# A retention layer and two MLPs on one core: the first loads throttled to 1 MB under way, two weight tiles decoded by halves, half of the first products moved ahead of the last attention, evacuations in pairs

## The chip, the cores and the metric

The kernel runs on one core of a Trainium2 chip. The metric is the device time of one launch in microseconds (us). Before the change it is 880.4 us, the median of three runs (880.11 to 880.4).

## The reference, cut to what matters

```
scores = q k^T / sqrt(64)                      # batch 4, 8 heads, 576 positions, head 64, f32
ret    = scores * gamma_h^(i-j) for j <= i     # a decay in place of a softmax
x      = (ret v) as 2304 tokens x 512
h = x @ moe_w_in;   x = max(0.01 h, h) @ moe_w_out        # 512 -> 2048 -> 512
h = x @ moe2_w_in;  out = (h * sigmoid(h)) @ moe2_w_out
```

q, k, v and x are f32; the four weight matrices arrive as 64-bit numbers and are decoded to f32 on the core.

## The kernel before, in words

**Engines.** PE is the matrix engine, DVE the vector engine, ACT the scalar engine, POOL a third elementwise engine; SP only issues DMAs. Each runs its own list in order, so an instruction that waits holds up all that stands behind it on its engine. The first part of the program, up to the end of the first two token blocks (`FIXED` steps), keeps the order in which it is written; what comes later is ordered by a scheduler.

**Attention.** The tokens of each of the four batches are cut into a unit A (256) and a unit B (320). A unit is worked off in two groups g of two head pairs p: `scale_k` multiplies a copy of the keys by decays, `products` makes the small 64x64 products (tile `r`: scores and key-value sums), DVE masks them (`pt`) and chains the states (`first`, `st`, `sa`), `outer` and `values` make the output (tile `o`), and DVE writes it to `X`. Units u0 = A of batch 0 and u1 = A of batch 1 come ahead of everything else (lines 449 to 509). They are the 512 tokens of the first block. Their q, k, v arrive as 16 loads of 256 KB (`qkvk`). The six other units are spread between the steps of the MLP; `attend` issues their parts when the step counter has passed a due time, and their loads (`qkv`, 672 KB each for a unit B) have due times too (0.3, 0.8 and 1.3 steps for the first three).

**MLP.** A block of up to 512 tokens is worked off in 16 steps, one for each tile f of 128 hidden units. At step t PE makes `gemm1` of tile t (12 products of 128x512 into `h`: hi and lo parts of x and of the weight in three passes over four chunks c) and `gemm2` of tile t-2 (12 products into `acc`). A product needs its operands split in two: `xs`, `wi`, `wo`, `g` each hold a part "hi" (a cast on ACT) and a part "lo" (a subtraction on DVE, for a few on POOL). The second product of a pass group needs the lo part of x or g, the third the lo part of the weight.

**Weights.** A tile f of both matrices is 1 MB in 64-bit form, loaded into one of three buffers `w64` by two DMAs of 512 KB. `decode` turns it into f32: ACT (line 319), DVE (324, 334), ACT again for a share `by_act` of the columns (330), DVE (337, 340). In block 0, at step t ACT and DVE decode tile t+2, split its `wi` half, make g of tile t and split `wo` of tiles t-1 and t. In order on ACT: 319, the activation `hs` of step t, 330, `g`, `wi`, `wo`. On DVE: 324, 334, 337, the lo part of `wo`, 340, then the lo parts of `g` and `wi`. A `w64` buffer is loaded again when the decode of the tile in it is over.

**Fillers.** `busy` issues products whose result nobody reads.

Of the kernel before, what the change touches and what calls it, by code (L numbers as in the profile page):

```python
# [24 lines left out]
BUSY = 3  # L25
# [39 lines left out]
def retention_mlp_kernel(ctx: ExitStack, tc: tile.TileContext, qkva, qkvb, w1, w2, consts, out):  # L65
# [76 lines left out]

    def load(u, p):

        k, b = u
        n, nv = (CA, 2) if k == "A" else (CB, 3)
        nq = n + 128 * nv
        m = nq + 128 * (nv + 2)
        src = (qkva if k == "A" else qkvb)[b, p]
        if u in UNITS[:2]:  # L150

            t = wraw_p.tile([128, m], F32, tag="wraw", name="qkvk")
            nc.sync.dma_start(out=t[:, :nq], in_=src[:, :nq])
            nc.sync.dma_start(out=t[:, nq:], in_=src[:, nq:])
        else:
            t = ld_p.tile([128, 1344], F32, tag="ld", name="qkv")
            nc.sync.dma_start(out=t[:, :m], in_=src)
        vk = t[:, nq:m].rearrange("p (k h d) -> p k h d", h=2, d=64)
        raw[u, p] = t[:, :n], t[:, n:nq], vk[:, :nv], vk[:, nv:]
# [11 lines left out]
    def products(u, ps):  # L171
# [23 lines left out]
        for p in ps:  # L195
            pt = pt_p.tile([128, 2, nm, CH], F32, tag="pt", name="pt")
            nc.vector.tensor_tensor(
                out=pt, in0=s[p].rearrange("p j (m n) -> p j m n", n=CH),
                in1=mask[:, 2 * p:2 * p + 2].unsqueeze(2).to_broadcast([128, 2, nm, CH]), op=ALU.mult)
# [21 lines left out]
        if first:  # L221
            last[u, ps] = t[:, 1, o:o + 256].rearrange("p (i n) -> p i n", i=2)[:, :, 64:]

# [71 lines left out]
    def load_w(layer, f):  # L295

        if layer == 1 and f < 2:
            w = ld_p.tile([128, 1024], F32, tag="ld", name="wraw")
        else:
            w = wraw_p.tile([128, 1024], F32, tag="wraw", name="wraw")  # L300
        wraw[layer, f] = w
        r = dec_p.tile([128, 1024, 2], I32, tag="w64", name="w64")
        src = (w1, w2)[layer][f].bitcast(I32)
        halves = [slice(0, 512), slice(512, 1024)]
        loads = []
        for c in halves:
            loads.append(nc.sync.dma_start(out=r[:, c].rearrange("p n t -> p (n t)"), in_=src[:, 2 * c.start:2 * c.stop]))
        for c in halves if (layer, f) == (0, 0) else [slice(0, 1024)]:
            wdec.append((w[:, c], r[:, c]))
        return loads[0]  # L310
# [32 lines left out]
    def split_wi(layer, i, f):  # L343

        w = wi_p.tile([128, 2, 512], F32R, tag="wi", name="wi")
        wsp[layer, i, f, 0] = w
        return split(w[:, 0], w[:, 1], wraw[layer, f][:, :512], nc.gpsimd if (layer, i, f) == (0, 0, 0) else nc.vector)
# [42 lines left out]
    def gemm2(layer, i, f):  # L390
        p0, n = BLOCKS[layer][i]
        nt = KC if layer == 0 else n // 128
        if f == 0:
            t = [acc_p.tile([128, 2, 512], F32, tag=f"acc{m}", name=f"acc{m}") for m in range((nt + 1) // 2)]
            acc[layer, i] = [t[m // 2][:, m % 2] for m in range(nt)]
        g, w = gs[layer, i, f], wsp[layer, i, f, 1]
        for m in range(nt):
            a = acc[layer, i][m]
            ms = slice(m * 128, (m + 1) * 128)
            for wa, ga in PASSES:  # L400
                st = f == 0 and (wa, ga) == (0, 0)
# [5 lines left out]
            if f < NF - 1:  # L407
                yield
                continue
            if layer == 0:  # L410
                if m % 2:
                    nc.vector.tensor_copy(out=X[:, m, p0:p0 + n], in_=a[:, :n])
                else:
                    nc.scalar.copy(out=X[:, m, p0:p0 + n], in_=a[:, :n])  # L414
            else:
                y = y_p.tile([128, 512], F32, tag="y", name="y")
                if m % 2:
                    nc.vector.tensor_copy(out=y, in_=a)  # L418
                else:
                    nc.scalar.copy(out=y, in_=a)  # L420
                for o, ln, r in rows_of(p0 + m * 128, 128):
                    nc.sync.dma_start(out=out[r:r + ln], in_=y[o:o + ln])
            yield


    nw = 0

    def more_weights(upto, x=None):
        nonlocal nw
        while nw < min(upto, 2 * NF):  # L430
            y = load_w(nw // NF, nw % NF)
            if x is not None:
                behind(y, x)
                x = None
            nw += 1

    def decodes():
        while wdec:
            run(decode(*wdec.pop(0)))
# [3 lines left out]
    nc.vector.memset(warm[:, :1], 0.0)  # L443
# [4 lines left out]
    ordered.enter_context(tc.manual_schedule())  # L448
    u0, u1 = UNITS[:2]
    nc.sync.dma_start(out=cst, in_=consts)  # L450
    more_weights(1)
    for g in range(NG):
        for u in (u0, u1):
            for p in (2 * g, 2 * g + 1):
                load(u, p)
    nc.vector.tensor_tensor(
        out=mask, in0=mask, in1=gn_sb.unsqueeze(2).to_broadcast([128, H, CH]), op=ALU.mult)
    decodes()
    more_weights(2)
# [5 lines left out]
    def sums(u, g):  # L465
        products(u, (2 * g, 2 * g + 1))

    t = ps_p.tile([128, 512], F32, tag="ps", name="busy")

    def busy(n):  # L470

        for _ in range(n):
            mm(t[:, :256], mask[:, 0:2], mask[:, 0:4], True, True)
# [7 lines left out]
    leave(u0, (0, 1))  # L481
    outer(u0, 0)
    values(u0, 0)
    sums(u1, 0)
    leave(u1, (0, 1))
    outer(u1, 0)
    sums(u0, 1)
    leave(u0, (2, 3))
    x = values(u1, 0)

    more_weights(4, x)
    for c in range(2):
        split_x(0, 0, c)
    outer(u0, 1)
    busy(1)
    sums(u1, 1)
    second = decode(*wdec.pop(0), 1024)
# [8 lines left out]
    busy(BUSY)  # L506
    for c in range(2, KC):
        split_x(0, 0, c)
    leave(u1, (2, 3))
# [5 lines left out]
    for u, a, z in ATT:  # L515
# [20 lines left out]
    for t, (l, i, f) in enumerate(steps):  # L536
        first = t < FIXED
        if t == 0:
            run(second)
            more_weights(5)  # L540
            run(split_wi(*steps[1]))
        for n, _ in enumerate(gemm1(l, i, f)):
            attend(t + (n + 1) / 8)
        a = activate(l, i, f)
        if first:

            d = decode(*wdec.pop(0), 512) if t + 2 < NF else iter(())
# [26 lines left out]
        if first:  # L574
            run(wi)
            if ends_block:
                next(wo)
# [15 lines left out]
        if t == FIXED - 1:  # L593
            ordered.close()
# [62 lines left out]
```

## Time and profile before

| | |
|---|---|
| median of 3 runs | 880.4 us |
| profiled execution, its own time | 880.94 us |
| span of its records | 879.2 us |
| PE busy | 855.6 us (97%) |
| DVE busy | 535.3 us (61%) |
| ACT busy | 442.8 us (50%) |
| bytes read from HBM | 53.09 MB |

How to read it: PE is the engine that everything ends on, and its share is an average. The first 80 us (attention of two units, then the block in which the weights are decoded) are a stage of their own, in which DVE, ACT and the DMA queue are busy too; behind it PE has next to no gap. Matrix products overlap each other, so the time of one (its latency) is longer than the distance between two.

### The profile page before, as it was taken

The numbers are of one execution on the slowest core, as the hardware profiler recorded it, in microseconds if no ns is written. First come the engines' busy times: TensorE is split into PE (matmuls) and PEld (weight loads), VectorE is DVE, ScalarE is ACT, GpSimd is POOL, SyncE is SP. The second block draws the span as 40 slices with busy tenths as digits, with TensorE's granted clock in tenths as the row PEclk, the third lists the DMA queues.
The fourth block names the chain that finished last, engine by engine and source line by source line (L and its number), as shares of the span: only waits on it lengthen the run. The fifth ranks groups of instructions, "written<-read, shape, count | busy, mean of one in ns | idle before, by whom it ended". The sixth has DMA issues, their size and how long they took to land.

```text
span 879.2 us, 14579 instructions
## 1 busy us (share of the span) xinstructions
PE 855.6 (97%) x6000; PEld 717.5 (82%) x6000; DVE 535.3 (61%) x928; ACT 442.8 (50%) x766; POOL 10.5 (1%) x27
## 2 busy tenths in 40 slices
PE   4899999999999999999999999999999999999997
PEld 4578778998877877888999888888888888888896
DVE  4688875576455564446999554654465445544575
ACT  2687754454333443445666444544454445444564
POOL 2100000000000000000000000000000000000000
PEclk9999999999999999999999999999999999999999
DMA  7576541221012010101561000010001000100010
GB/s 294 205 258 229 186 160 57 87 83 57 1 59 87 24 52 30 48 1 48 193 238 49 1 0 1 1 48 1 1 1 48 1 0 1 48 1 0 25 25 25
DMA packets 17826, 58.75 MB, mean 67 GB/s; under 512 B 2016, under 2 KB 2144, under 8 KB 17760
## 3 DMA queue, kind: packets, MB, share of 16 engines
q1 hardware_dynamic: 17760, 57.82, 18.8%
q8 instruction: 47, 0.77, 0.4%
q14 instruction: 19, 0.16, 0.1%
HBM read 53.09 MB, written 4.72 MB: 66 GB/s over the span
## 4 chain that ended last, share of the span: by engine, by line
PE 91%; DVE 1%; ACT 1%; issue 0%; DVEq 0%
PE acc L129 44%; PE h L129 43%; PE o L129 2%; PE r L129 2%; DVE wraw L340 0%; ACT X L414 0%; DVE st L231 0%; DVE g L108 0%; DVE y L418 0%; ACT g L107 0%; ACT wo L107 0%; DVE wi L108 0%; ACT hs L384 0%; ACT y L420 0%; DVE xs L108 0%
## 5 line engine op out<-in xcount | busy, mean ns | idle before, releaser
L129 PE MATMUL h<-xs,wi 128*128 128x512 f32 (+3 forms) x1920 | 432.6, 370 | 1.9 <-ACT wi L107 1.8
L129 PEld LDWEIGHTS h<-xs,wi 128*128 128x128 f32 x1920 | 341.9, 188 | 61.5 <-ACT wi L107 2.7
L129 PE MATMUL acc<-g,wo 128*128 128x512 f32 (+2 forms) x960 | 218.4, 372 | 1.4 <-ACT X L414 1.4
L129 PE MATMUL acc<-wo,g 128*128 128x512 f32 x864 | 212.8, 390 | 0.7 <-ACT y L420 0.7
L129 PEld LDWEIGHTS acc<-g,wo 128*128 128x128 f32 x960 | 171.5, 188 | 28.7 <-ACT X L414 2.2
L129 PEld LDWEIGHTS acc<-wo,g 128*128 128x128 f32 x864 | 161.0, 188 | 33.8 <-ACT y L420 1.1
L107 ACT CAST wo<-wraw 128x512 fp32r<-128x512 f32 x160 | 99.4, 621 | 136.4 <-PE acc L129 136.2
L108 DVE TENSOR_TENSOR wo<-wraw,wo 128x512 fp32r<-128x512 f32 x160 | 110.4, 690 | 94.2 <-ACT wo L107 93.5
L108 DVE TENSOR_TENSOR wi<-wraw,wi 128x512 fp32r<-128x512 f32 x159 | 109.2, 687 | 54.0 <-ACT wi L107 51.9
L387 DVE TENSOR_TENSOR hs<-h,hs 128x512 f32<-128x512 f32 (+1 forms) x80 | 51.0, 638 | 107.2 <-ACT hs L386 107.1
L108 DVE TENSOR_TENSOR g<-hs,g 128x512 fp32r<-128x512 f32 (+3 forms) x160 | 101.6, 635 | 17.0 <-ACT g L107 12.9
L386 ACT ACTIVATE hs<-h 128x512 f32<-128x512 f32 (+1 forms) x80 | 44.4, 555 | 122.2 <-PE h L129 122.0
L107 ACT CAST wi<-wraw 128x512 fp32r<-128x512 f32 x160 | 98.1, 613 | 15.2 <-DVE wraw L340 15.2
L107 ACT CAST g<-hs 128x512 fp32r<-128x512 f32 (+3 forms) x160 | 93.5, 584 | 11.2 <-DVE hs L387 10.6
L384 ACT ACTIVATE hs<-h 128x512 f32<-128x512 f32 (+2 forms) x80 | 44.3, 554 | 107.1 <-PE h L129 104.6
L319 ACT ACTIVATE wraw<-w 128x1024 f32<-128x1024 f32 (+1 forms) x33 | 36.7, 1111 | 14.5 <-DVE wo L108 8.3
L324 DVE TENSOR_SCALAR w<-w 128x512 uint16<-128x512 uint32 (+1 forms) x32 | 33.5, 1047 | 12.1 <-ACT wraw L319 12.0
L340 DVE SCALAR_TENSOR_TENSOR wraw<-w,wraw 128x1024 int32<-128x1024 int32 (+1 forms) x33 | 39.3, 1190 | 1.6 <-ACT w L330 1.4
L107 ACT CAST xs<-X 128x512 fp32r<-128x512 f32 (+3 forms) x40 | 22.7, 578 | 6.5 <-DVE X L275 5.1
L108 DVE TENSOR_TENSOR xs<-X,xs 128x512 fp32r<-128x512 f32 (+3 forms) x38 | 23.5, 635 | 3.3 <-ACT xs L107 3.1
L330 ACT ACTIVATE w<-w,seven 128x512 uint16<-128x512 uint32 (+1 forms) x15 | 23.0, 1535 | 0.0
L129 PEld LDWEIGHTS r<-qkv 64*64 64x64 f32 x896 | 15.5, 134 | 8.2 <-issue 4.6
(55 smaller groups left out, 241.4 us busy)
## 6 DMA issues: line engine op xcount, KB each, us to landing
w<-in_w SPq DMA_DIRECT2D x64, 512.0 KB, 4.6
qkv<-in_qkvb SPq DMA_DIRECT2D x16, 672.0 KB, 5.4
qkvk<-in_qkva SPq DMA_DIRECT2D x16, 256.0 KB, 5.2
qkv<-in_qkva SPq DMA_DIRECT2D x8, 512.0 KB, 4.3
out<-y SPq DMA_DIRECT2D x15, 256.0 KB, 2.0
out<-y SPq DMA_DIRECT2D x6, 128.0 KB, 2.4
cst<-in_consts SPq DMA_DIRECT2D x1, 138.0 KB, 2.2
```

The source lines that it names most:

```text
L107: yield nc.scalar.copy(out=hi, in_=src)
L108: yield engine.tensor_tensor(out=lo, in0=src, in1=hi.bitcast(F32), op=ALU.subtract)
L129: return nc.tensor.matmul(out, lhsT, rhs, start=start, stop=stop)
L319: yield nc.scalar.mul(out=w, in_=hi.bitcast(F32), mul=2.0 ** -112)
L324: yield nc.vector.tensor_scalar(out=end[:, c], in0=lo[:, c].bitcast(U32), scalar1=2.0 ** -29, scalar2=7.0, op0=ALU.mult, op1=ALU.min)
L330: yield nc.scalar.activation(out=end[:, c], in_=lo[:, c].bitcast(U32), func=AF.Relu, scale=-2.0 ** -29, bias=seven)
L340: yield nc.vector.scalar_tensor_tensor(out=wi, in0=hi, scalar=-0x7FFFFFF9, in1=wi, op0=ALU.bitwise_and, op1=ALU.bitwise_xor)
L384: yield nc.scalar.activation(out=hs[:, :n], in_=h[:, :n], func=AF.Prelu, alpha=0.01)
L386: yield nc.scalar.activation(out=hs[:, :n], in_=h[:, :n], func=AF.Sigmoid)
L387: yield nc.vector.tensor_tensor(out=hs[:, :n], in0=h[:, :n], in1=hs[:, :n], op=ALU.mult)
```

## The change

It has six parts. (1) Every load goes through `fetch`, which as long as `limit` holds (to the end of step 31) makes a load wait, on SP, until all but 1 MB of the loads before it and itself have landed. (2) Tile 1 is loaded and decoded in two halves (its `wi` half, then its `wo` half), tile 2 too; the `wo` halves are decoded at the end of steps 0 and 1, all of their columns in line 350 (`by_act` 512 of 512). (3) Two of the four chunks of the first step's `gemm1` are issued ahead of `outer` of the last group of u1. (4) The copy `first` goes to ACT, one `wi` subtraction to POOL, and the fillers read a tile that is set at the start, four of them ahead of everything. (5) `scale_k` has its due time 0.05 steps behind the step before it, where it was half an interval. (6) `acc` tiles are evacuated in pairs, and a block of 256 tokens has an `acc` tile of its own for each half.

```
+AWAY = 4 << 18
...
+    away = []
+
+    def fetch(out, in_):
+
+        y = nc.sync.dma_start(out=out, in_=in_)
+        size = 4 * math.prod(out.shape)
+        if limit:
+            while away and sum(z for _, z in away) + size > AWAY:
+                x = away.pop(0)[0]
+                if not away or sum(z for _, z in away) + size <= AWAY:
+                    behind(y, x)
+            away.append((y, size))
+        return y
...
-            nc.vector.tensor_copy(out=st, in_=t[:, 0, o:o + 256].rearrange("p (i n) -> p i n", i=2)[:, :, :64])
+            nc.scalar.copy(out=st, in_=t[:, 0, o:o + 256].rearrange("p (i n) -> p i n", i=2)[:, :, :64])
...
+        for i in parts:
+            y = fetch(w64[layer, f][:, i * 512:(i + 1) * 512].rearrange("p n t -> p (n t)"),
+                      src[:, i * 1024:(i + 1) * 1024])
+            if x is not None:
+                behind(y, x)
+        if len(parts) == 2:
+            wdec.append((wraw[layer, f], w64[layer, f]))
...
-            t = [acc_p.tile([128, 2, 512], F32, tag=f"acc{m}", name=f"acc{m}") for m in range((nt + 1) // 2)]
-            acc[layer, i] = [t[m // 2][:, m % 2] for m in range(nt)]
+            t = [acc_p.tile([128, 2, 512], F32, tag=f"acc{m}", name=f"acc{m}") for m in range(2)]
+
+            acc[layer, i] = [t[m // 2][:, m % 2] if nt > 2 else t[m][:, 0] for m in range(nt)]
...
+            if f == NF - 1 and (m % 2 or nt < 3):
+                for e in (m,) if nt < 3 else (m - 1, m):
+                    evacuate(layer, p0, n, e, acc[layer, i][e])
...
+    for n, (f, i) in enumerate(((2, 0), (1, 1), (2, 1))):
+        load_w(0, f, (i,), x if n == 0 else None)
+    split_x(0, 0, 0)
+    leave(u0, (2, 3))
+    values(u0, 1)
+    second = half(1, 0, 512)
     next(second)
+    split_x(0, 0, 1)
     next(second)
-    busy(2)
-    values(u0, 1)
+    h0 = gemm1(0, 0, 0)
+    next(h0)
+    next(h0)
     outer(u1, 1)
-    next(second)
-    busy(2)
+    run(second)
     values(u1, 1)
...
-                queue.append((at + d / 2, (f, x)))
+                queue.append((at + 0.05, (f, x)))
...
+            if t == 0:
+                more_weights(4)
+                d = half(2, 0, 0)
...
         if first:
             run(wi)
+            if t < 2:
+                run(half(1 + t, 1, 512))
```

Three places show how the lists change. The first is PE's list at the end of the attention of u0 and u1, as one piece of the difference: `r` is `products` of group 1 of u1, the first run of `o` rows `values` of u0, the second `outer` and `values` of u1.

```order
 L129 MATMUL r<-qkvk 64x64 x32
-L129 MATMUL busy<-mask 128x256 x2
 L129 MATMUL o<-pt,qkvk 64x64 x8
 L129 MATMUL o<-qkvk,first 64x64 x4
 L129 MATMUL o<-qkvk,st 64x64 x4
 L129 MATMUL o<-qkvk,sa 64x64 x4
-L129 MATMUL o<-pt,qkvk 64x64 x8
-L129 MATMUL busy<-mask 128x256 x2
-L129 MATMUL o<-pt,qkvk 64x64 x8
+L129 MATMUL h<-xs,wi 128x512 x6
+L129 MATMUL o<-pt,qkvk 64x64 x16
```

Six of the first step's twelve products now stand between `values` of u0 and `outer` of u1; 30 of them (36 before) follow behind.

The second place is SP's list of loads before the change, from the buffer of tile 4 (`w_529`) over tile 5 (`w_561`) to tile 6 (`w_599`); `qkv` are the first three loads of unit B of batch 0, and the brackets name the semaphores waited for (a DMAHW semaphore counts landed DMAs).

```order
L307 DMA w_529<-in_w 128x1024 [waits DMAHW2_49]
L157 DMA qkv<-in_qkvb 128x1344
L307 DMA w_561<-in_w 128x1024 [waits DMAHW6_49,DMAHW5_49,DVE_49]
L307 DMA w_561<-in_w 128x1024
L157 DMA qkv<-in_qkvb 128x1344
L157 DMA qkv<-in_qkvb 128x1344 [waits DMAHW7_49]
L307 DMA w_599<-in_w 128x1024 [waits DMAHW0_49,DVE_49]
L307 DMA w_599<-in_w 128x1024 [waits DMAHW1_49]
```

The same place in the change (tile 4 is `w_556`, tile 5 `w_560`, tile 6 `w_604`):

```order
L147 DMA w_556<-in_w 128x1024 [waits DMAHW0_49]
L147 DMA w_560<-in_w 128x1024 [waits DMAHW1_49,DVE_49]
L147 DMA w_560<-in_w 128x1024 [waits DMAHW2_49]
L147 DMA qkv<-in_qkvb 128x1344 [waits DMAHW4_49]
L147 DMA qkv<-in_qkvb 128x1344 [waits DMAHW5_49]
L147 DMA qkv<-in_qkvb 128x1344 [waits DMAHW6_49]
L147 DMA w_604<-in_w 128x1024 [waits DMAHW7_49,DVE_49]
L147 DMA w_604<-in_w 128x1024
```

All three `qkv` loads now stand behind tile 5, and the semaphores 4, 5, 6 and 7 are those of the load just ahead of each: the second half of tile 5, then each `qkv` in turn.

The third place is ACT's list behind the last `xs` casts, before (tile 2 is `w_384`, tile 3 `w_388`) and in the change (tile 1 is `w_147`, tile 2 `w_447`, tile 3 `w_544`):

```order
L319 ACTIVATE wraw<-w_384 128x1024
L384 ACTIVATE hs<-h 128x512
L330 ACTIVATE w_384<-w_384,seven 128x512
L107 CAST g<-hs 128x512
L107 CAST wi<-wraw 128x512
L107 CAST wo<-wraw 128x512
L319 ACTIVATE wraw<-w_388 128x1024
```

```order
L339 ACTIVATE wraw<-w_447 128x512
L404 ACTIVATE hs<-h 128x512
L107 CAST g<-hs 128x512
L107 CAST wi<-wraw 128x512
L107 CAST wo<-wraw 128x512
L339 ACTIVATE wraw<-w_147 128x512
L350 ACTIVATE w_147<-w_147,seven 128x512
L339 ACTIVATE wraw<-w_544 128x1024
```

Step 0 has lost half of the first instruction and all of the third; the second half of tile 1 now stands ahead of tile 3, and that of tile 2 ahead of tile 4 one step later.

## Rows read from the trace of the kernel before

**Rows 1.** Page, busy time of each engine: us, share of the span, instructions.

```profile
PE 855.6 (97%) x6000; PEld 717.5 (82%) x6000; DVE 535.3 (61%) x928; ACT 442.8 (50%) x766; POOL 10.5 (1%) x27
```

**Rows 2.** Page, a costly group (mean ns); windows: busy us by engine, clock, DMA share, GB/s.

```profile
L107 ACT CAST wi<-wraw 128x512 fp32r<-128x512 f32 x160 | 98.1, 613 | 15.2 <-DVE wraw L340 15.2
...
100.00:200.00 100.00, 98.53 (x1196) 87.11 (x1195) 68.57 (x147) 51.49 (x93) 0.92 (x5) 1.00 0.30 103
```

**Rows 3.** Timeline, 14 to 41 us: start, us, instruction, idle time before it.

```profile
14.26 1.88 PE L129 MATMUL r<-qkvk 64*64 64x64 f32 x64
...
19.87 1.44 PE L129 MATMUL r<-qkvk 64*64 64x64 f32 x43 [2.05 <-issue]
...
24.20 1.16 PE L129 MATMUL r<-qkvk 64*64 64x64 f32 x64 [0.64 <-DVE done L246]
24.88 2.52 POOL L108 TENSOR_TENSOR xs<-X,xs 128x512 fp32r<-128x512 f32 x2 [6.99 <-ACT xs L107]
...
26.42 2.62 ACT L330 ACTIVATE w<-w,seven 128x1024 uint16<-128x1024 uint32 x1
...
30.66 0.27 PE L129 MATMUL o<-qkvk,first 64*64 64x64 f32 x1 [1.69 <-issue]
...
32.30 3.11 PE L129 MATMUL h<-xs,wi 128*128 128x512 f32 x12
...
40.53 3.30 PE L129 MATMUL h<-xs,wi 128*128 128x512 f32 x12 [1.53 <-ACT wi L107]
```

**Rows 4.** DMA queues from 17 to 18 us: packets, MB, share of 16 engines.

```profile
q1 hardware_dynamic: 113, 0.41, 100.1%
q8 instruction: 1, 0.02, 5.9%
```

**Rows 5.** Windows: stretch, length, busy us of five engines, granted clock, DMA share, GB/s.

```profile
16.00:19.30 3.30, 1.18 (x44) 0.85 (x38) 2.00 (x8) 0.27 (x1) 1.23 (x2) 1.00 0.91 364
19.40:22.70 3.30, 2.83 (x100) 2.83 (x99) 1.21 (x4) 0.00 (x0) 0.00 (x0) 0.50 0.04 12
```

**Rows 6.** Timeline of PE, steps 4 to 6.

```profile
51.89 1.52 PE L129 MATMUL h<-xs,wi 128*128 128x512 f32 x6
...
58.30 2.88 PE L129 MATMUL h<-xs,wi 128*128 128x512 f32 x12
...
63.89 0.74 PE L129 MATMUL r<-qkv 64*64 64x64 f32 x16 [1.52 <-ACT qkv L165]
...
66.75 2.89 PE L129 MATMUL h<-xs,wi 128*128 128x512 f32 x12
```

**Rows 7.** Timeline of ACT and DVE, steps 0 and 4.

```profile
37.07 1.45 ACT L330 ACTIVATE w<-w,seven 128x512 uint16<-128x512 uint32 x1
...
57.47 1.13 ACT L319 ACTIVATE wraw<-w 128x1024 f32<-128x1024 f32 x1
...
60.54 0.69 DVE L108 TENSOR_TENSOR wo<-wraw,wo 128x512 fp32r<-128x512 f32 x1
```

**Rows 8.** Timeline of SP: issues of loads, 40 to 80 us.

```profile
40.65 0.91 SPq L157 DMA_DIRECT2D qkv<-in_qkvb  x2
45.17 34.98 SPq L307 DMA_DIRECT2D w<-in_w  x14
```

**Rows 9.** Loads near 12.0, 68.2 and 74.4 us, KB, us to landing; line 157 to 150.

```profile
qkvk<-in_qkva SPq DMA_DIRECT2D x1, 256.0 KB, 5.1
...
w<-in_w SPq DMA_DIRECT2D x1, 512.0 KB, 3.7
...
w<-in_w SPq DMA_DIRECT2D x1, 512.0 KB, 4.9
...
DMA to landing us min/median/max: 4.1/6.5/9.8
```

**Rows 10.** Waits over the whole span: engine, line, releaser, us in total, times, longest.

```profile
PE acc L129 <- ACT X L414: 1.4, 2, 0.7
...
PE acc L129 <- ACT y L420: 0.7, 1, 0.7
```

More of the change, by code (lines that the diff above doesn't have):

```diff
@@ L293, in retention_mlp_kernel, with load_w, half @@
     acc = {}
[L295 to L302, printed above, removed]
-        src = (w1, w2)[layer][f].bitcast(I32)
[L304 to L310, printed above, removed]
+    w64 = {}
+    def load_w(layer, f, parts=(0, 1), x=None):
+        if (layer, f) not in w64:
+            p, tag = (ld_p, "ld") if layer == 1 and f < 2 else (wraw_p, "wraw")
+            wraw[layer, f] = p.tile([128, 1024], F32, tag=tag, name="wraw")
+            w64[layer, f] = dec_p.tile([128, 1024, 2], I32, tag="w64", name="w64")
+        src = (w1, w2)[layer][f].bitcast(I32)
+        for i in parts:
[5 more added lines that the diff above has]
+            wdec.append((wraw[layer, f], w64[layer, f]))
+    def half(f, i, by_act):
+        c = slice(i * 512, (i + 1) * 512)
+        return decode(wraw[0, f][:, c], w64[0, f][:, c], by_act)
     def decode(w, r, by_act=0):
@@ L346, in split_wi @@
         wsp[layer, i, f, 0] = w
[L347 removed]
+        return split(w[:, 0], w[:, 1], wraw[layer, f][:, :512], nc.gpsimd if (layer, i) == (0, 0) and f < 2 else nc.vector)
     def split_wo(layer, i, f):
@@ L406, in gemm2, with evacuate, more_weights @@
                     mm(a, g[:, wa, ms], w[:, ga], st, sp)
[L407 to L422, printed above, removed]
-            yield
-    nw = 0
-    def more_weights(upto, x=None):
+            if f == NF - 1 and (m % 2 or nt < 3):
+                for e in (m,) if nt < 3 else (m - 1, m):
+                    evacuate(layer, p0, n, e, acc[layer, i][e])
+            yield
+    def evacuate(layer, p0, n, m, a):
+        if layer == 0:
+            y = X[:, m, p0:p0 + n]
+            a = a[:, :n]
+        else:
+            y = y_p.tile([128, 512], F32, tag="y", name="y")
+        if m % 2:
+            nc.vector.tensor_copy(out=y, in_=a)
+        else:
+            nc.scalar.copy(out=y, in_=a)
+        if layer == 1:
+            for o, ln, r in rows_of(p0 + m * 128, 128):
+                nc.sync.dma_start(out=out[r:r + ln], in_=y[o:o + ln])
+    nw = 3
+    limit = True
+    def more_weights(upto):
         nonlocal nw
         while nw < min(upto, 2 * NF):
[L431 to L434, printed above, removed]
+            load_w(nw // NF, nw % NF)
             nw += 1
@@ L448, in retention_mlp_kernel, with busy @@
     ordered.enter_context(tc.manual_schedule())
+    t = ps_p.tile([128, 512], F32, tag="ps", name="busy")
+    def busy(n, size=256):
+        for _ in range(n):
+            mm(t[:, :size], warm[:, :128], warm[:, :size], True, True)
     u0, u1 = UNITS[:2]
     nc.sync.dma_start(out=cst, in_=consts)
-    more_weights(1)
+    load_w(0, 0, (0,))
+    load_w(0, 0, (1,))
     for g in range(NG):
@@ L455, in retention_mlp_kernel @@
                 load(u, p)
+    load_w(0, 1, (0,))
+    busy(4, 512)
     nc.vector.tensor_tensor(
         out=mask, in0=mask, in1=gn_sb.unsqueeze(2).to_broadcast([128, H, CH]), op=ALU.mult)
-    decodes()
-    more_weights(2)
+    for i in range(2):
+        run(half(0, i, 0))
     def scales(u, g):
@@ L465, in sums @@
     def sums(u, g):
[L466 to L473, printed above, removed]
+        return products(u, (2 * g, 2 * g + 1))
     scales(u0, 0)
@@ L481, in retention_mlp_kernel @@
     leave(u0, (0, 1))
+    busy(1)
     outer(u0, 0)
+    busy(1)
     values(u0, 0)
@@ L485, in retention_mlp_kernel @@
     leave(u1, (0, 1))
+    busy(1)
     outer(u1, 0)
     sums(u0, 1)
[L488 to L493, printed above, removed]
+    values(u1, 0)
     outer(u0, 1)
     busy(1)
-    sums(u1, 1)
-    second = decode(*wdec.pop(0), 1024)
+    x = sums(u1, 1)
+    for n, (f, i) in enumerate(((2, 0), (1, 1), (2, 1))):
[4 more added lines that the diff above has]
+    second = half(1, 0, 512)
     next(second)
+    split_x(0, 0, 1)
     next(second)
-    busy(2)
-    values(u0, 1)
+    h0 = gemm1(0, 0, 0)
+    next(h0)
+    next(h0)
     outer(u1, 1)
-    next(second)
-    busy(2)
+    run(second)
     values(u1, 1)
-    busy(BUSY)
+    leave(u1, (2, 3))
+    wi1 = split_wi(0, 0, 1)
+    next(wi1)
+    busy(3)
     for c in range(2, KC):
         split_x(0, 0, c)
-    leave(u1, (2, 3))
+    run(wi1)
     steps = [(l, i, f) for l in range(2) for i in range(len(BLOCKS[l])) for f in range(NF)]
@@ L537, in retention_mlp_kernel @@
         first = t < FIXED
[L538 to L542, printed above, removed]
+        for n, _ in enumerate(h0 if t == 0 else gemm1(l, i, f)):
             attend(t + (n + 1) / 8)
@@ L593, in retention_mlp_kernel @@
         if t == FIXED - 1:
+            limit = False
             ordered.close()
```

15 lines of the change are left out of this document (8 added, 7 removed).

## The prediction

> **What bounds the kernel now.** The page first: PE is busy for 855.6 of 879.2 us [rows 1]. Then the windows: from 100 to 200 us PE lacks 1.47 of 100 us [rows 2], and 1.37 of these are one kind of wait (6. below). So behind the first steps PE sets the time alone, and an edit pays only by what it takes out of the first 65 us or out of those few gaps. The timeline of the first part shows what stands there. The first MLP product begins at 32.30 us, tile 2's products at 40.53 us behind a wait of 1.53 us for the cast of `wi` [rows 3]. Ahead of that PE stops twice for about 2 us with nothing but "issue" named, up to 19.87 and up to 30.66 us [rows 3]. In the first stop's last part of data the queues show why: from 17 to 18 us the loads take the 16 DMA engines fully, and one packet of PE's instructions lies among them [rows 4]. I read the stops as PE waiting for instructions that stand behind 2 MB of data.
>
> **1. Up to `products` of the last group (24.20 us before).** The first products are bound by their loads either way: the last load that they need is issued a little later under the limit but meets a shorter queue. Three things move the path from there.
> - The first stop. A 256 KB load takes 5.1 us to land [rows 9] with eight of them under way; with four it should be near half. If the instruction packet waits like a load, it comes some 2.4 us earlier; the stop, which begins earlier too, shrinks from 2.05 to about 1: -1.0 (bounds 0 and -2.05).
> - PE's clock. The same 64 products take 1.88 us at 14 us and 1.16 us at 24 us [rows 3]. A stretch with 1.18 of 3.30 us busy is followed by one at a granted clock of 0.50, the lower of the two levels, 1.2 GHz [rows 5]. The fillers keep PE busy from the start. Two such batches and some 40 products of `values` lie on the path, so at most -0.72 x 2 - 0.6 = -2.0; I take -1.4.
> - The copy `first` on ACT must wait for `pt` on DVE and then DVE for it: an estimated 0.15 each in four rounds, +0.6.
>
> Sum -1.8: `products` of the last group at 22.4 instead of 24.20. The Trainium skill ("TensorE: Matmul & The Clock Gate", Part 1) says that idleness closes PE's clock gate and activity opens it. The pair of windows in rows 5 agrees; by that rule in full the clock term would be -2.0 rather than -1.4.
>
> **2. From there to tile 2.** Before, 24.20 to 40.53 is 16.3 us. After: products 1.16, `pt` and `first` together an estimated 1.1, a cast of 0.6 for `xs` [rows 2], then two subtractions on POOL at 1.26 each (half of 2.52) [rows 3] with an ACT instruction between them, so the half `gemm1` ends near 28.5. PE's list is in order, so `outer` and `values` of u1, ready long before, wait behind it and end at 29.9. `X`, two casts (0.6 each) and two subtractions (0.69 each, [rows 7]) later the second half runs to 33.2; tile 1's twelve products, 2.75 or so [rows 6], to 35.95. What was late before is early now: line 330 of tile 1 covers 512 columns, not 1024 (2.62 us to about 1.45) [rows 3, 7], so `wi` of tile 1 is there by 32, and that of tile 2, whose line 330 is gone from step 0 altogether, by 35.8. The second stop should vanish, since no load is under way when its packet is asked for. Tile 2's products: about 36.0, 4.5 us ahead of 40.53 (34 if the first stop vanishes, 39 if stop and clock stay as they are).
>
> **3. The halves come back.** The `wo` halves of tiles 1 and 2 are decoded at the ends of steps 0 and 1, with all 512 columns in line 350: on ACT 0.65 (half of line 319's 1.13 and its start) + 1.2 (1.45 with its overlap) [rows 7], on DVE an estimated 1.05, ahead of tiles 3 and 4. ACT's list for step 1 becomes 1.85 longer, its `g`, `wi` and `wo` are late by it, and the lo part of `wo` on DVE, which the third product of `gemm2` needs, too. Following both lists: `gemm2` of tile 0 resumes at 40.4 and tile 3's `gemm1` begins at 43.0; `gemm2` of tile 1 resumes at 47.65 and tile 4's `gemm1` begins at 50.1, against 51.89 [rows 6]. Of the 4.5 us 1.8 are left.
>
> **4. The loads stand behind each other.** This term decides. Before, the last two of the three `qkv` loads were issued at 40.65 and tile 6 at 45.17, several under way together [rows 8]; ACT turned to tile 6 at 57.47, 12.3 us later [rows 7]. In the change `limit` holds until step 31, and two loads of 672 KB do not fit in 1 MB. So each `qkv` waits for the load ahead of it to land, and tile 6 for the third `qkv`. Prices are those of loads that found the queue empty: 512 KB 3.7, a pair together about 5.0 (the second of one took 4.9 from its own issue), 672 KB 4.1, the shortest of its line [rows 9].
> Tile 4's buffer is free when the second half of tile 1 is decoded, at 38.55; its halves land at 42.3 and 43.5. The halves of tile 5 follow each, the second at 47.3. Then three times 4.1 and 0.05 for the wait: 51.4, 55.6, 59.75. Tile 6: 59.8, landed 64.8 to 65.0. That is 26.4 us behind the issue of tile 4, against some 19.5 that the steps leave. ACT, which would take tile 6 at about 58, stops for 7 us. Behind it on ACT stand `hs` of step 4, `g`, `wi` of tile 6; on DVE 324, 334, 337 of tile 6 and behind them the lo part of `wo` of tile 3, over about 3.05 after ACT's start (57.47 to 61.23 before [rows 7], of which 0.7 was other work on DVE). PE, in order, reaches the third product of `gemm2` of tile 3 at about 60.8 and goes on at 68.05. With ten products at 0.23 (2.88 for twelve) [rows 6] and the `products` of the second pair (0.75) tile 6's `gemm1` begins at 71.1, against 66.75 [rows 6]: **+4.35**. In this sum the wait of 1.52 us before 63.89 for line 165 [rows 6] is gone already, since (5) puts that scale a step earlier, where its load (55.6) is there. The later tiles need 4 to 5 us for each MB and a step lasts more (51.89 to 58.30 is 6.4 [rows 6]), so the queue catches up; DVE, now without lead, costs PE perhaps 0.5 more (0 to 1).
>
> The Trainium skill ("DMA: Bandwidth & Descriptors", Anatomy of one DMA) gives a fixed cost of about 2.0 us and 436 GB/s, fitted for another path; that estimate is 3.6 for 672 KB and 3.2 for 512 KB, under the 4.1 and 3.7 of rows 9. By it the chain would be some 3 us shorter and the sum about +1.3. The rows decide.
>
> **5. The clock behind that stop.** PE would idle about 7 us. The stretch behind the 2.05 us stop, 3.3 us, stood at 0.50 [rows 5]; a like stretch of full-width products costs half its length, 1.6. Taken +1.5 (0 if the clock holds, 3.3 if it is low for twice as long).
>
> **6. Evacuations.** At the end of block 0 PE waits for the copy of the first half of an `acc` tile before it may write the other half: two waits, 1.4 us (0.68 each in the timeline), and at the very end one more of 0.7 [rows 10]. With pairs and tiles of their own these three go: -2.05. The copies then run beside products of the other tile. Bound on the other side 0.
>
> **Sum.** +4.35 + 0.5 + 1.5 - 2.05 = +4.3 us. The profiled execution took 880.94 us (879.2 of span and 1.7 around it), 0.5 over the median 880.4; the difference goes to the median: 884.7.
>
> **Rivals.**
> - *Faster: the loads keep up.* If tile 6 has landed when ACT turns to it, at about 58, there is no stop. It decides at a chain of 19.5 us from tile 4 to tile 6 instead of 26.4. For it: bandwidth is 364 GB/s and more when the queue is full [rows 5], at which 672 KB are 1.9 us, and the lone prices come from few rows. Against: of the nine loads of line 157 in 150 us none landed in under 4.1 [rows 9]. Then the 1.8 us of step 3 stay, the 1.52 of rows 6 go, and the evacuations: 880.4 - 1.8 - 1.5 - 2.05 = 875.
> - *No change: the stop is small.* At 3.3 us for each link the chain is about 21.5, the stop near 2 us and hardly a change of clock: tile 6 a little before 66.75, in all 879 to 881.
> - *Slower still: the head gains nothing.* If the clock stays low and the stops stay, tile 2 begins at 39, and the chain, which starts from it, slides by 3: 887.7. For it: the loads fill the first 18 us [rows 4], and the four long fillers, at the lower clock, may still run when the first data arrive.
>
> **How the numbers follow.** A measurement of this kernel tells 0.2%, 1.8 us. My forecast (the stop at tile 6, 881.5 to 888 with its bounds) 0.45; the worse head 0.13; no change 0.19; the loads keep up 0.23. Of the forecast's own range little lies under 882.2. So slower 0.6, same 0.18, faster 0.22. The range that leaves out 2 in 10 reaches down into the faster case and up to the worse head: 876.5 to 888.5.
>
> **What would show it.** Right: a PE idle of 5 to 8 us behind `acc` before tile 6's `gemm1`, with the lo part of `wo` as its releaser, ACT's line 339 waiting for a weight DMA, SP's three `qkv` issues about 4.1 us apart; tile 2's `gemm1` near 36; no gap at the end of block 0; the granted clock lower for a few us behind the stop. Wrong: `qkv` issues closer than 3.3 us, or tile 2 before 33, which would leave the head more than the chain takes back; or stops in later blocks, of which I see no cause.

## The result and the profile after

The change makes the kernel slower: 890.78 us (median of 4 runs, 888.63 to 892.39) beside 880.26 us, a ratio of 1.0118 with a 95% interval from 1.0095 to 1.0141. The forecast was slower, by the stop that came, but 884.7 us with a range to 888.5. The profiled execution took 890.01 us (span 888.3), 9.1 us more than that of before.

The page of the change first: busy time, and the costliest group that waits (busy us, mean ns | idle before it, releaser).

```profile
PE 863.2 (97%) x6006; PEld 720.6 (81%) x6006; DVE 537.6 (61%) x926; ACT 446.9 (50%) x773; POOL 11.8 (1%) x28
...
L129 PE MATMUL acc<-g,wo 128*128 128x512 f32 (+2 forms) x960 | 219.2, 375 | 11.7 <-DVE wo L108 11.7
```

`gemm2` has 11.7 us of waits for the lo part of `wo`. PE's timeline says where (start, us, instruction, idle time before it and its releaser):

```profile
22.27 0.93 PE L129 MATMUL r<-qkvk 64*64 64x64 f32 x48 [1.01 <-DVE done L261]
...
25.87 0.50 PE L129 MATMUL h<-xs,wi 128*128 128x512 f32 x1 [1.16 <-ACT xs L107]
...
27.22 0.95 PE L129 MATMUL h<-xs,wi 128*128 128x512 f32 x3 [0.85 <-POOL xs L108]
...
31.72 2.93 PE L129 MATMUL busy<-warm 128*128 128x256 f32 x6
...
34.08 7.84 PE L129 MATMUL h<-xs,wi 128*128 128x512 f32 x30
41.76 0.61 PE L129 MATMUL acc<-g,wo 128*128 128x512 f32 x2
43.76 2.56 PE L129 MATMUL acc<-g,wo 128*128 128x512 f32 x10 [1.39 <-DVE wo L108]
46.16 2.88 PE L129 MATMUL h<-xs,wi 128*128 128x512 f32 x12
...
51.06 2.60 PE L129 MATMUL acc<-g,wo 128*128 128x512 f32 x10 [1.57 <-DVE wo L108]
53.50 1.52 PE L129 MATMUL h<-xs,wi 128*128 128x512 f32 x6
56.03 1.18 PE L129 MATMUL r<-qkv 64*64 64x64 f32 x40 [1.00 <-DMA qkv<-in_qkvb]
...
59.75 2.58 PE L129 MATMUL acc<-g,wo 128*128 128x512 f32 x10 [0.51 <-DVE wo L108]
...
73.70 0.79 PE L129 MATMUL acc<-g,wo 128*128 128x512 f32 x1 [8.20 <-DVE wo L108]
74.42 1.35 PE L129 MATMUL r<-qkv 64*64 64x64 f32 x40
75.70 4.21 PE L129 MATMUL acc<-g,wo 128*128 128x512 f32 x9
79.70 2.99 PE L129 MATMUL h<-xs,wi 128*128 128x512 f32 x12
```

Both stops of [rows 3] with only "issue" named are gone, and the products of the last group begin at 22.27 us. Tile 2's products, the last twelve of the thirty, end when `acc` begins at 41.76 and take 2.72, so they began near 39.0: only 1.5 us of the head's gain is left. Two waits for `wo` follow, of 1.39 and 1.57 us, one of 1.00 us for the first `qkv` load, and one more for `wo` of 0.51 us. Then comes the stop of 8.20 us, and tile 6 begins at 79.70 where it was 66.75 [rows 6]: 12.95 us late.

Why PE stops is read from the two lists that it ends on. ACT first:

```profile
61.91 0.69 ACT L179 ACTIVATE qkv<-qkv,cst 128x128 f32<-128x128 f32 x2
70.57 1.12 ACT L339 ACTIVATE wraw<-w 128x1024 f32<-128x1024 f32 x1 [7.96 <-DMA w<-in_w]
```

Then SP's issues of loads (the second figure is the time that the group's issues span):

```profile
41.59 5.92 SPq L147 DMA_DIRECT2D w<-in_w  x4
52.17 9.62 SPq L147 DMA_DIRECT2D qkv<-in_qkvb  x3
65.46 5.37 SPq L147 DMA_DIRECT2D w<-in_w  x4
```

And what SP waited for from 36 to 72 us (us in total, times, longest):

```profile
SPq L147 <- DMA qkv<-in_qkvb: 12.2, 3, 5.1
```

ACT stands 7.96 us for the load of tile 6. That load was issued at 65.46, when the third `qkv` had landed; each `qkv` was issued when the one ahead had landed; the first of them at 52.17, behind tile 5. From tile 4's issue to ACT's start on tile 6 it is 28.98 us. Before, the last two `qkv` loads and the first half of tile 6 went out within 4.6 us [rows 8].

The DMA view of the change from 52 to 66 us, the time of the three `qkv` loads, shows what one load at a time costs (40 slices: busy tenths of the DMA engines, GB/s; then the queue of the loads: packets, MB, share):

```profile
DMA  0009369996000092679931100000049699841000
GB/s 0 0 0 154 77 246 384 430 399 277 0 0 0 0 262 77 246 323 399 438 138 46 46 15 31 15 0 0 0 92 200 215 430 415 369 184 61 0 0 0
...
q1 hardware_dynamic: 432, 2.06, 44.9%
```

Three humps, one for each `qkv`, with stretches of nothing between them: a load moves most of its data in seven or eight slices of 0.35 us and takes 3.8 to 5.4 us to land, and under the limit nothing else uses the rest. The DMA engines are busy for 44.9% of these 14 us, and tile 6, for which ACT and then PE will stop, is not asked for before their end.

Windows of the change (stretch, length, busy us of PE, PEld, DVE, ACT, POOL, granted clock, DMA share, GB/s), around the early half of the first products and around the stop:

```profile
24.80:28.40 3.60, 1.45 (x4) 0.67 (x4) 1.78 (x6) 3.37 (x7) 2.51 (x2) 1.00 0.61 187
28.40:31.80 3.40, 3.11 (x59) 2.16 (x59) 1.11 (x3) 0.36 (x2) 0.02 (x1) 0.53 0.73 265
31.80:35.20 3.40, 3.40 (x8) 2.77 (x9) 2.66 (x5) 2.07 (x4) 1.27 (x1) 0.50 0.86 266
...
73.70:77.00 3.30, 3.30 (x44) 2.55 (x45) 2.37 (x3) 2.41 (x5) 0.00 (x0) 0.50 0.65 222
77.00:80.40 3.40, 3.40 (x10) 2.63 (x10) 3.36 (x6) 2.50 (x5) 0.00 (x0) 0.59 0.71 233
```

PE is busy for 1.45 of 3.60 us while it waits for the parts of `xs` from ACT and POOL, and the next two stretches run almost wholly at the lower level, 1.2 GHz (0.53 and 0.50). So do, for the most part, the two behind the long stop (0.50 and 0.59).

### The profile page after: what moved, and what is told of

It reads as the page before. It is cut to its first block, busy times and chain, and to the rows that moved or that the text cites. A ratio compares the mean times of both kernels' runs of the same rounds, so it can differ in the third digit from the quotient of the medians.

```text
span 888.3 us, 14605 instructions
## 1 busy us (share of the span) xinstructions
PE 863.2 (97%) x6006; PEld 720.6 (81%) x6006; DVE 537.6 (61%) x926; ACT 446.9 (50%) x773; POOL 11.8 (1%) x28
## 2 busy tenths in 40 slices
DMA packets 17826, 58.75 MB, mean 66 GB/s; under 512 B 2016, under 2 KB 2144, under 8 KB 17760
## 4 chain that ended last, share of the span: by engine, by line
PE 89%; DVE 1%; DMA 1%; ACT 0%; SPq 0%; issue 0%
PE acc L129 43%; PE h L129 42%; PE o L129 2%; PE r L129 2%; DMA qkv<-in_qkvb 1%; SPq L147 0%; ACT w L350 0%; DVE wraw L360 0%; DVE wi L108 0%; DVE wo L108 0%; DVE st L246 0%; DVE xs L108 0%; DVE y L440 0%; DVE g L108 0%; ACT hs L404 0%; DVE pt L211 0%
## 5 line engine op out<-in xcount | busy, mean ns | idle before, releaser
L129 PE MATMUL acc<-g,wo 128*128 128x512 f32 (+2 forms) x960 | 219.2, 375 | 11.7 <-DVE wo L108 11.7
L129 PE MATMUL acc<-wo,g 128*128 128x512 f32 x864 | 210.0, 390 | 0.0
L107 ACT CAST wi<-wraw 128x512 fp32r<-128x512 f32 x160 | 98.1, 613 | 14.5 <-DVE wraw L360 14.5
L360 DVE SCALAR_TENSOR_TENSOR wraw<-w,wraw 128x1024 int32<-128x1024 int32 (+1 forms) x35 | 39.6, 1133 | 4.5 <-ACT w L350 4.2
L350 ACT ACTIVATE w<-w,seven 128x512 uint16<-128x512 uint32 x16 | 23.2, 1451 | 0.1
L129 PEld LDWEIGHTS r<-qkv 64*64 64x64 f32 x896 | 15.6, 138 | 7.3 <-issue 4.9
```

Source lines behind the costliest of these rows:

```text
L107: yield nc.scalar.copy(out=hi, in_=src)
L129: return nc.tensor.matmul(out, lhsT, rhs, start=start, stop=stop)
L350: yield nc.scalar.activation(out=end[:, c], in_=lo[:, c].bitcast(U32), func=AF.Relu, scale=-2.0 ** -29, bias=seven)
L360: yield nc.vector.scalar_tensor_tensor(out=wi, in0=hi, scalar=-0x7FFFFFF9, in1=wi, op0=ALU.bitwise_and, op1=ALU.bitwise_xor)
```

## The experiments

My theory after this result: the limit makes one chain of the loads behind tile 4, and that chain is the whole loss; the head gains less than forecast because of the early half; and the pairs give back more than forecast. Rivals: the `wo` halves that are decoded late, or the order of `qkv` behind tile 5, make the loss. Times are medians; each ratio stands against runs of the kernel before on the same chip.

### The limit ends behind the head (e1), and no limit (e2)

```
# e1, at step 0, ahead of the loads of tile 3
+                limit = False
# e2
-    limit = True
+    limit = False
```

> The limit of 1 MB holds for the attention's loads and the weights of tiles 0 to 2 alone; from tile 3 on every load is issued when its buffer is free, all else as in the change. Theory (the one-at-a-time chain from tile 5 over the three qkv loads to tile 6 makes the stop): the stop of 8.2 us ahead of tile 6 and the low clock behind it vanish, tile 6's products begin at 66 to 68 us, and with the cheaper evacuations the time is 876 to 880. Rival A (the wo halves decoded at the ends of steps 0 and 1 make ACT and DVE late, whatever the loads): PE still stops for over 4 us ahead of tile 6, time 886 to 890. Rival B (the order, with qkv behind tile 5, is what makes tile 6 late): as rival A in time, but ACT would wait for tile 6's load and not for its own work.

> No limit on the loads at all, all else as in the change. Theory: the chain is gone as in the run before; in the head PE's two stops with only issue named should come back, if they were instructions waiting behind full queues: some 1 to 2 us of stop ahead of products of the last group, which then begins at 22.5 to 24 us. Time 876 to 881, that is within 2 us of the run with the limit in the head alone. Rival (the stops come from something else, such as the short fillers or the copy of the first state): products of the last group begin at 22.3 as in the change and no issue stop over 1 us shows.

Measured: e1 877.19 us, ratio 0.9962 (0.9949 to 0.9975); e2 876.50 us, 0.9955 (0.9940 to 0.9969). So the limit behind the head costs 13.6 us (890.78 - 877.19), and rivals A and B fall: halves and order are as in the change. SP's timeline in e1:

```profile
41.30 4.10 SPq L147 DMA_DIRECT2D w<-in_w  x4
45.44 1.90 SPq L147 DMA_DIRECT2D qkv<-in_qkvb  x3
48.62 21.27 SPq L147 DMA_DIRECT2D w<-in_w  x10
```

Tile 4 is issued at the same time as in the change, and tile 6 at 48.62 in place of 65.46. PE's timeline in e1 at that place:

```profile
62.32 0.86 PE L129 MATMUL acc<-g,wo 128*128 128x512 f32 x3
...
66.04 2.89 PE L129 MATMUL h<-xs,wi 128*128 128x512 f32 x12
```

No stop, and tile 6 begins at 66.04. In e2 the head's stop came back as foreseen: the group of `products` before the last one resumes like this,

```profile
18.48 1.09 PE L129 MATMUL r<-qkvk 64*64 64x64 f32 x58 [1.04 <-issue]
```

while in e1 and in the change none shows there. It does not show in the time: e2 is no slower than e1. The second stop of [rows 3], the one at 30.66 us, shows neither in e2 nor in e9, both without a limit, so it is not the limit that took it away. Under the limit the loads themselves end later (below).

### Without the early half (e3), and without both (e9)

```
-    next(h0)
-    next(h0)
     outer(u1, 1)
...
     run(wi1)
+    next(h0)
+    next(h0)
```

> The first step's products all stand behind the last attention again, all else as in the change. Theory (in the change PE waits inside the early half for the lo parts of xs from ACT and POOL, so outer and values of the last group are late and PE falls to the low clock for 7 us): without it tile 2's products begin 1.5 to 3 us earlier, at 36 to 38 us. The chain of loads starts from tile 2's decode, so the gain at the end is the same or less: 887.5 to 890. Rival (the head is bound by ACT and DVE, the decode of tile 1, and not by PE's order): tile 2 begins within 0.7 us of 39.2 and the time is that of the change, 890 to 891.

> The change with no limit at all and with all of the first step's products behind the last attention. Theory (the early half costs 3.5 us in the change by itself, by PE's waits inside it and the low clock behind them, and limit and early half act apart): 873 to 875, against 876.5 with the early half. Rival (without the limit the head is bound by ACT and DVE, so that the order on PE is worth nothing): 876 to 877.5.

Measured: e3 887.32 us, 1.0082 (1.0066 to 1.0099), 3.5 us under the change; e9 872.78 us, 0.9922 (0.9907 to 0.9936), 3.7 us under e2. Each of the four stands against the kernel before on its own chip; by these ratios the two differences are 3.2 and 2.9 us (0.0036 and 0.0033 of 880). The intervals of the first pair just touch, those of the second stand apart. So the early half costs about 3 us, with the limit and without. PE's timeline in e3:

```profile
24.07 1.16 PE L129 MATMUL r<-qkvk 64*64 64x64 f32 x64 [1.01 <-DVE done L261]
...
30.18 1.99 PE L129 MATMUL h<-xs,wi 128*128 128x512 f32 x7
32.90 6.90 PE L129 MATMUL h<-xs,wi 128*128 128x512 f32 x29 [0.74 <-DVE xs L108]
39.64 0.61 PE L129 MATMUL acc<-g,wo 128*128 128x512 f32 x2
```

From the last group's `products` to the end of tile 2's it is 15.6 us here (24.07 to 39.64) and 19.5 in the change (22.27 to 41.76). The whole head of e1 is the same list as that of the change, and took 18.0 (23.44 to 41.43) at a granted clock of 0.70, 0.81 and 1.00 in the three stretches where the change has 1.00, 0.53 and 0.50. In e3 it was 1.00 from 24 to 39.6 us. So of the 3.9 us some 1.5 or more go with the clock; the other 2.4 are the order together with what the low clock cost in e1. Single executions, so an estimate.

### Evacuations in pairs alone, on the kernel before (e4, and a second look)

The edit is the part of the change in `gemm2` with `evacuate`, and nothing else.

> The kernel before with the evacuations in pairs and a tile of its own for each half of a block of 256 tokens, and nothing else of the change. Theory (the evacuation is worth what lies between 3.85 us, the distance that the change wins back behind tile 6's products, and 2.05 us, the waits that the trace of before names): 876.5 to 878.3. Rival (part of the 3.85 us is the later due time of the scales or slack that the late start of the change leaves): 878 to 878.8.

Measured: 876.29 us, 0.9961 (0.9947 to 0.9974), that is -3.9 us, just under the range of the theory; the interval leaves out the rival. The end of block 0 before the change, from the first 128x320 product of the next block to the first behind the evacuation:

```profile
129.08 2.32 PE L129 MATMUL h<-xs,wi 128*128 128x320 f32 x12
...
139.25 1.65 PE L129 MATMUL acc<-g,wo 128*128 128x512 f32 x6 [0.68 <-ACT X L414]
...
142.38 1.47 PE L129 MATMUL h<-xs,wi 128*128 128x320 f32 x9
```

and in e4:

```profile
127.37 2.32 PE L129 MATMUL h<-xs,wi 128*128 128x320 f32 x12
...
138.81 1.48 PE L129 MATMUL h<-xs,wi 128*128 128x320 f32 x9
```

13.30 us became 11.44: the two waits of 0.68 [rows 10], and 0.5 more that stands with no wait of its own. From there to the end e4 is 1.5 us shorter (735.3 beside 736.8 us). That makes 3.4 us behind tile 6. The other 1.7 us by which the two profiled executions differ lie ahead of tile 6, where the stops at "issue" of e4 were shorter, and are not the evacuations. The run below is the same kernel once more, in spite of its name.

> The kernel with the evacuations in pairs alone, a second look. Theory (the two stops with only issue named change from execution to execution, 2.05 and 1.69 us in the first profile, 0.69 and 0.67 in the second of the same list): again under 1 us or near 2 us each, and the first product of tile 6 between 64 and 67 us accordingly. Rival (they have a fixed size set by the list): 0.6 to 0.8 us each.

Measured: 875.38 us (one run). The two stops at "issue" took 1.11 and 1.16 us, in e4 0.69 and 0.67, in the first profile 2.05 and 1.69 [rows 3], all with the same list up to there. They change from execution to execution, and no single profile gives their price.

### The limit alone, on the kernel before (e5)

The edit is `fetch` with `AWAY` and `limit`, and the loads that go through it.

> The kernel before with the limit of 1 MB on its loads to the end of step 31, and nothing else of the change. Theory (the limit costs what the change loses: the change is 13.6 us longer than the run whose limit ends behind the head): ACT waits 5 to 10 us for tile 6's load, PE stops as long, and the time is 888 to 895. Rival (the limit hurts only together with the halves and with qkv behind tile 5, that is in the change's order of loads): a stop under 4 us, 879 to 884.

Measured: 891.34 us, 1.0117 (1.0097 to 1.0137): the limit alone costs 11.3 us, as much as the change loses. Its ACT waits for tile 6 as in the change, with one `qkv` load ahead of tile 5:

```profile
65.77 1.12 ACT L334 ACTIVATE wraw<-w 128x1024 f32<-128x1024 f32 x1 [7.53 <-DMA w<-in_w]
```

PE's stop at this place is 5.02 us, with 0.96 more for line 180 behind it. The rival, that the limit hurts only with the halves and the new order, falls.

### The stop filled with work (e6)

```
+        for c in 3 * list(range(KC)) if (layer, i, f) == (0, 0, 5) else ():
+            for a, e in PASSES:
+                mm(h[:, :n], w[:, a, c * 128:(c + 1) * 128], xs[layer, i, c][:, e, :n], ...
```

> The change with the twelve products of tile 5's gemm1 made four times (three times more than needed, with the same result), so that PE works through its stop of 8.2 us: 36 more products at 0.24 us are 8.5 us. Theory (the stop lowers the clock, and the 52 products behind it take 6.0 us in place of 3.0): the stretch behind the stop takes 3.0 to 3.3 us and the time falls by 2 to 3 us against the change, to 887.8 to 888.8. Rival (those products are slow for another reason, their operands or the loads that land beside them): the stretch stays near 6 us and the time is 890.5 to 891.5.

Measured: 888.72 us, 1.0098 (1.0080 to 1.0116), 2.1 us under the change; the two intervals overlap, so the medians alone do not show it. PE's timeline in e6:

```profile
64.37 11.05 PE L129 MATMUL h<-xs,wi 128*128 128x512 f32 x48
75.25 0.84 PE L129 MATMUL acc<-g,wo 128*128 128x512 f32 x3
76.02 0.81 PE L129 MATMUL r<-qkv 64*64 64x64 f32 x40
76.77 2.34 PE L129 MATMUL acc<-g,wo 128*128 128x512 f32 x9
78.94 2.88 PE L129 MATMUL h<-xs,wi 128*128 128x512 f32 x12
```

From 76.02 to 78.94, `products` and the nine, it is 2.92 us; in the change 5.28 (74.42 to 79.70). With PE kept at work the granted clock in 70 to 77 us was 1.00, and the same operands, with the same loads beside them, go at full speed. ACT began on tile 6 at 71.94 us in e6, later than in the change:

```profile
71.94 1.12 ACT L339 ACTIVATE wraw<-w 128x1024 f32<-128x1024 f32 x1 [7.16 <-DMA w<-in_w]
```

From there to the products of tile 6 it is 7.00 us, in the change 9.13. So the clock behind the stop is worth 2.1 to 2.4 us of the loss by the timelines, and the medians agree.

### 2 MB under way (e7), and that without the early half (e10)

```
-AWAY = 4 << 18
+AWAY = 8 << 18
```

> The change with 2 MB under way in place of 1 MB: a tile and half of the next, or three qkv of 672 KB, then go together. Theory (the loss is one load at a time): tile 6 is there before ACT turns to it at about 62.6 us, no stop, and the time is that of the run whose limit ends behind the head, 876 to 879. Rival (any wait between loads is dear, by its own delay or by what SP cannot issue meanwhile): a stop of 2 to 5 us remains, 880 to 886.

> The change with 2 MB under way and with all of the first step's products behind the last attention. Theory (the 2 MB limit costs nothing and the early half costs its 3.5 us whatever the limit): 871 to 873.5, at or a little under the run without any limit. Rival (the gain of 2 MB over no limit, 875.0 against 876.5, is real and adds up): under 871.5. Rival (2 MB does cost something that the early half hid): 874 to 876.

Measured: e7 874.99 us, 0.9944 (0.9929 to 0.9959); e10 873.44 us, 0.9921 (0.9905 to 0.9936). ACT in e7:

```profile
57.83 1.12 ACT L339 ACTIVATE wraw<-w 128x1024 f32<-128x1024 f32 x1 [0.45 <-DMA w<-in_w]
```

Twice the limit removes the stop: three loads of 672 KB (2016 KB) fit under it. A wait between loads is not dear by itself; one load at a time is. e7 is not told apart from e2, nor e10 from e9. The early half costs 1.6 us here by the medians and 2.0 us by the ratios; the two intervals overlap, so this is not told apart from the 3 us of the other two pairs.

### Pairs and the due time (e12)

```
-                queue.append((at + d / 2, (f, x)))
+                queue.append((at + 0.05, (f, x)))
```

> The kernel before with evacuations in pairs and with the due time of the scales 0.05 of a step behind the step before. Theory (the later due time makes the wait of 1.5 us for line 165 ahead of 63.89 us): no wait, 874.5 to 875.2 against 876.3 with the pairs alone. Rival (the scale then waits for its load, or DVE is late instead): 876 to 877.5.

Measured: 875.61 us, 0.9944 (0.9925 to 0.9963). The wait of 1.5 us for line 165 is gone from PE's timeline; that the time fell by 0.7 us against e4 lies within the two intervals, so the gain is not shown.

### The late halves without line 350 (e13), and with no limit or one in the head (e14, e15)

```
-                run(half(1 + t, 1, 512))
+                run(half(1 + t, 1, 0))
```

e13 has 2 MB and no early half besides, e14 no limit, e15 2 MB up to the loads of tile 2.

> The run with 2 MB and no early half, and the two late halves decoded without line 350 on ACT (by_act 0 of 512 in place of 512 of 512, so that DVE's line 344 makes all of their columns). Theory (the halves cost PE 3.0 us, two waits of 1.4 and 1.6 us for wo, since line 350 holds ACT for 1.2 us and DVE waits 1.06 us for it in each): each wait falls by some 0.75 us, the time by 1 to 1.5 us against that run. Rival (DVE is the bound there, so its added 0.55 us in each half is paid): the waits stay and the time is the same or up to 1 us longer.

> The run without line 350 in the late halves, and no limit at all. Theory (with 2 MB the 1.4 us that the halves gave back ended as a wait of 1.59 us for tile 6, since its load still stood behind the qkv loads by the limit): tile 6 is loaded as soon as its buffer is free, the wait falls under 0.5 us, and the time is 871 to 872.5. Rival (the buffer, the bandwidth of nine loads in a row, and not the limit, hold tile 6): a wait of 1 us or more for tile 6 stays, 872.5 to 874.

> The same with 2 MB for the loads of the attention and of tiles 0 to 2 and no limit from tile 3 on. Theory: as the run with no limit, 871 to 872.5, with less of a stop at issue in the head if that limit keeps instructions from waiting behind data. Rival (as above): 872.5 to 874.

Measured: e13 872.72 us, 0.9922 (0.9903 to 0.9941); e14 872.88 us, 0.9920 (0.9906 to 0.9934); e15 872.53 us, 0.9915 (0.9900 to 0.9929). PE's timeline in e13:

```profile
39.16 2.57 PE L129 MATMUL acc<-g,wo 128*128 128x512 f32 x10 [0.69 <-DVE wo L108]
...
45.69 2.58 PE L129 MATMUL acc<-g,wo 128*128 128x512 f32 x10 [0.79 <-DVE wo L108]
...
59.46 0.49 PE L129 MATMUL acc<-g,wo 128*128 128x512 f32 x1 [1.59 <-DVE wo L108]
```

Both waits fell by 0.7 and 0.8 us, as the theory had it, and the time did not: 1.59 us came back at tile 6, since everything but its load was earlier. The clock fell behind this wait too: in e13 the nine products of `gemm2` ahead of tile 6 took 3.6 us, with a granted clock of 0.57 from 60.6 to 64.3 us, in e14 2.2 us. In e14 that wait is

```profile
58.39 0.50 PE L129 MATMUL acc<-g,wo 128*128 128x512 f32 x1 [0.23 <-DVE wo L108]
```

and in e15 0.54 us. So the 2 MB still held tile 6 there, not its buffer. The profiled spans follow (872.8, then 870.8 and 870.9 us), the medians do not, and e13's profiled execution was 1.9 us over its own median; what this gives of the time is under what these runs can tell. The times of e14 and e15 lie just above the 871 to 872.5 us of the theory; it is the wait that speaks for it. The stop at "issue" in the head was not shorter with a limit there (1.43 us in e15, 1.25 in e14). e15 has the lowest median of the study, 0.85% under the kernel before by the ratio, and e9, e10, e13 and e14 are not told apart from it.

## Why the prediction was wrong in size

The profiled executions differ by 9.1 us, the medians by 10.5; the forecast was 4.3. What came was the mechanism that the prediction named, a chain of single loads that stops ACT and PE ahead of tile 6. What failed were the sizes of three of its terms: the head with the early half (step 2), the links of the chain (step 4) and the clock behind the stop (step 5). By its own steps, on the profiled executions:

1. **Up to the last group: a hit, in part by luck.** 22.4 forecast, 22.27 measured. But the same list up to there gave 23.44, 24.07 and 24.26 in e1, e3 and e6, and e2, without the limit, 22.51: the gain in the head changes from execution to execution, and none by the limit is shown. The parts of the sum were not right either: the first stop went whole, and the loads took longer under the limit (from 10 to 20 us 293 GB/s in place of 365), so waits of 0.60 and 0.46 us for scales on POOL took part of that back. The second stop vanished as forecast, but not for the reason given: loads were under way (DMA share 0.73 from 28.4 to 31.8 us), and it is gone without a limit too (e2).
2. **From there to tile 2: the step that failed first.** Tile 2 at 36.0 forecast, near 39.0 measured. I let `outer` and `values` wait behind the early half, but priced its own waits and the clock behind them too low: the half was to end near 28.5 and `values` at 29.9, and they ended at 29.5 and 31.7. e3 and e9 show the cost of the early half as about 3 us of the whole time: without it tile 2 begins at 36.9 in e3 (39.64 - 2.72).
3. **The halves: near.** From tile 2 to tile 4's products 14.1 us forecast (36.0 to 50.1), 14.5 measured. The two waits for `wo` are there, and e13 shows that line 350 on ACT makes about half of each.
4. **The chain: right in kind, too short.** The `qkv` loads go one at a time and ACT waits for tile 6 (7.96 us, forecast 7). From tile 4's issue to ACT's start on tile 6 28.98 us were measured, 26.4 forecast: tiles 4 and 5 took 10.6 in place of 8.75, and the `qkv` links 13.3 in place of 12.45. The larger part, 1.8 us, is thus in tiles 4 and 5: the second half of tile 5 was priced like a lone load, 3.8 us, but the first half was still under way beside it and it landed after 5.0; the second half of tile 4 landed 5.6 us behind the issue of the first, forecast 4.95. For the three `qkv` links I took one price, that of the shortest load of the line; the second took 5.4 with no other load of SP's under way. By the Trainium skill ("DMA: Bandwidth & Descriptors", Anatomy of one DMA), whose fit is for another path, such a load would take an estimated 3.6 us; the three took 3.8, 5.4 and 3.9 here, and the measurement decides. The 0.5 us for a DVE without lead did not show: PE has no wait with a named releaser from 79.70 to 140 us.
5. **The clock behind the stop: mis-sized.** +1.5 forecast with a bound of 3.3; the stretch took 3.0 longer (6.0 us from 73.70 to 79.70), and e6 gives back 2.1 to 2.4 of it (timelines).
6. **Evacuations: mis-sized.** -2.05 forecast from the named waits, -3.85 measured behind tile 6 in the change (12.95 late there, 9.1 at the end) and -3.4 behind tile 6 in e4. The other 0.45 of the change has no cause shown.

Sum of the misses: +3.0 (head) + 2.6 (chain) + 1.5 (clock) - 1.8 (evacuations) - 0.5 = +4.8, and 4.3 + 4.8 = 9.1. The range failed because three bounds that I held to be apart went the same way: the worse head, which I had as a rival at 0.13, starts the chain later and does not exclude the longer chain or the full price of the clock.

The rival on the other side, that the loads keep up, gave 875 us; it is what happens at 2 MB (e7, 874.99), where its condition holds.

What stays open: how much of the early half's cost is clock, and whether it is less at 2 MB. No run takes out alone the halves, the copy `first` on ACT or the new fillers, so what each of these is worth is not shown.

## What to carry to other kernels

A limit on the loads under way that lets several small loads go together makes a chain of large ones: work out for each load size how many fit, and follow the chain to the first engine that waits for its end. Here no limit gained time that these runs can tell, neither in the head alone (e1 beside e2) nor at 2 MB (e7 beside e2, e10 beside e9). An operation moved ahead on an engine that runs in order must have all its operands there, since its waits hold up what was ready behind it, and where the granted clock falls after them, as here, that costs again. An edit that removes a wait may give more than the wait that the trace names, here 1.86 us for 1.36 at the end of block 0.

## What the runs showed of the hardware that was not expected

With 1 MB under way the loads kept the DMA engines busy for 87.5% of the stretch from 10 to 20 us, and moved 293 GB/s; e2, the same list with no limit, had 87.2% and 338 GB/s, and the kernel before 93.2% and 365 GB/s. So the busy share says little about the rate. The loads of 256 KB issued in that stretch landed in 4.0 us (median; 3.7 in e1) in place of 5.1 before and 5.2 in e2: with 1 MB under way, by the prediction's count half of what it was before, the time to landing was far from half.

The second `qkv` load of the chain, alone in the queue, moved most of its data like the others, in seven slices, and then a rest at 15 to 46 GB/s for five more. It took 1.5 us longer to land than the other two. Nothing in the trace names a cause.

The stop at "issue" ahead of the last group had 0.69, 1.11 and 2.05 us in three executions of one list (e4, e11 and before), 1.04 to 1.88 in the seven runs of the change with no limit or 2 MB, and did not show at that place in the five with 1 MB. That fits instructions that wait behind data; no run moved the instructions themselves, so it is not shown.
